# 256 more columns of the first query weights stay in SBUF, and the feed-forward ring is cut into fewer, larger loads

## The chip, the core and the metric

The kernel runs on one core of one Trainium2 chip. The metric is device time in microseconds (us) of one execution, as a median over runs. Beside the times there is one profiled execution, whose trace gives the start and length of each instruction, of each wait and of each load.

## The reference

Two layers with the same weights, for four sequences of one new token each. Each layer is attention over a cache and then a gated feed-forward block:

```python
# B=4, D=640, 32 heads of 128, window of 1024 keys, F=1728, all float32
def _A_ref(x, k_cache, v_cache, wq, wo):
    q = heads_of(x @ wq)
    scores = jnp.einsum("bhqd,bhkd->bhqk", q, k) * (Dh ** -0.5)   # last 1024 keys
    p = _softmax(scores, axis=-1)
    o = jnp.einsum("bhqk,bhkd->bhqd", p, v)
    return merged(o) @ wo

def _B_ref(x, W_gate, W_up, W_down):
    gate = x @ W_gate; up = x @ W_up
    return (gate * (gate > 0) * up) @ W_down

x = x + _A_ref(_layernorm(x), ...);  x = x + _B_ref(_layernorm(x), ...)   # twice
```

Almost all of the work is reading: the last 1024 keys and values of 32 heads and 4 sequences, and the weights, once in each layer.

## The kernel before, in words

All inputs are laid out beforehand as rows of 128 partitions: `heads` (27 of the 32 heads: their columns of W_q, their keys, their values and their rows of W_o, in the order of use), `kept` (the same for the last five heads) and `mlp` (the feed-forward weights in the order of use). A length is counted here in floats per partition; a load of n floats moves 128 rows of n floats.

SBUF holds one large tile, `store` (STORE floats), through which everything streams, and `first_q` (HELD floats), which is loaded once and stays: the first 4608 floats of `heads`, which are the W_q columns of the first group of four heads and four of the five pieces of the second group's. Layer 1 doesn't load them again. The `kept` row stays in `store` as well: layer 0 takes these five heads last and layer 1 takes them first. Layer 0's feed-forward block therefore has little room. It streams its 25920 floats of `mlp` through a ring of seven places, 7040 floats in all: three beyond the kept row (z, f and f+1280 in the code), and four inside it (a = AHEAD, k and k+960 = BACK, q = AWAY). What stood in these four is parked meanwhile: AHEAD in `probs` and the tiles pT, BACK in the PSUM tiles ps, po and y, AWAY in the upper columns of the PSUM tiles pp and m.

A list `plan` has all loads in order. `load()` (L226) issues the next loads on SP's queue as long as the floats they overwrite are no longer marked live; `done()` (L279) unmarks them as TensorE's products have read them. The order of SP's queue is thus fixed by the plan, and each load waits for the product that read its place last. One part of head 17's values comes by small loads of 5, 2 or 1 rows (`limbs`, L238) into the last 2048 floats of `store`.

Groups of heads follow one another: `query`, `query_out` and `query_turned` make the query (TensorE, VectorE, TensorE), `scores` and `softmax` the weights, `values` and `project` the output. `normalized` and `deviation` (L378, L391) are the layer norm: the first gives the centered x in xT, the second the factor rstd, with a product over the partitions (`mean`) ahead of a square root.

The feed-forward block is `forward` (L585). `gate(j)` multiplies one of four pieces of W_gate and W_up (j = 3 first, with 128 columns to a product, then 0, 1, 2 with 256) into `gus[j]`, two halves of the tile pp in turn. `gated(j)` takes the rectified gate by ScalarE and the product with up by VectorE out of it, `hidden(j)` turns that, and `down(j)` multiplies by W_down into y. `fill` and `busy` (L361, L354) are products of the identity with itself into po that nobody reads; in layer 0's feed-forward block they stand at fixed places of TensorE's order.

Of the kernel before, what the change touches and what calls it, by code (L numbers as in the profile page):

```python
# [14 lines left out]
P = 128  # L15
# [11 lines left out]
KV = 4096  # L27
# [33 lines left out]
HELD = 4608  # L61
STORE = 50304
# [3 lines left out]
AHEAD = KEPT * D, KEPT * D + 1088  # L66
# [4 lines left out]
FIRST, MOST = 32128, 16064  # L71
LAP = 3 * MOST
SPLIT, PART = 17, 2048
LIMBS = [(half + i, 5, 0, 1536) for i in range(4) for half in (0, 32)] + [(i, 2, 1536, PART) for i in range(3)] + [(3, 1, 1536, PART), (7, 1, 1536, PART)]
# [39 lines left out]
def decode_kernel(ctx: ExitStack, tc: tile.TileContext, x, source, out):  # L114
# [29 lines left out]
    def stretch(layer, lo, end, to):  # L144

        loads = []
        for hi in fewest(lo, end, -(-(end - lo) // MOST))[1]:
            if to + hi - lo > LAP:
                to = 0
            loads.append((lo, hi, to))  # L150
            to, lo = to + hi - lo, hi
        last = next(i for i, (lo, hi, _) in enumerate(loads) if lo < at_part("v", SPLIT) + KV - 512 <= hi)
        for i, (lo, hi, at) in enumerate(loads):
            if last - 3 < i <= last:
                half = (i - last + 1) * 6 + 1
                plan.extend((layer, "limbs", p, p + 1, STORE - PART) for p in range(max(half, 0), half + 6))
            put(layer, "heads", at, lo, hi)
        return to
# [20 lines left out]
    put(0, "kept", k0, k0, k1, v0, v0 + 6656, v1, v1 + KV, v1 + 7168, FRONT)  # L179
    put(0, "kept", 0, 0, len(HEADS[K0]) * D, KEPT * D)  # L180


    f, z, a, q, k = FRONT, STORE - D, AHEAD[0], AWAY[0], BACK[0]
    assert STORE - FRONT == 1280 + 1024 + D
# [4 lines left out]
    for to, n in gu + gu + gu_end + wd:  # L189
        put(0, "mlp", to, lo, lo + n)  # L190
        lo += n
# [8 lines left out]
    for n in 832, 1280, 1024, 2048, 3392:  # L200
        to = put(1, "heads", to, lo, lo + n)
        lo += n
# [14 lines left out]
    cuts = [0, 7040, 12160, GU0 + 3 * GU, WD1 + WD, MLP - 4 * D, MLP - 2 * D, MLP - D, MLP - QUARTER, MLP]  # L217
# [33 lines left out]
    def place(layer, row, lo):  # L251

        if row == "heads" and lo < HELD:
            return first_q, lo, HELD - lo
        most = KV
        if row == "kept" and layer:
            if AHEAD[0] <= lo < AHEAD[1]:
                i = lo - AHEAD[0] - INSIDE
                if i < 0:
                    return probs, 1024 + i, -i  # L260
                return pT[i // P], GAP + i % P, min(P - i % P, AHEAD[1] - lo)
# [146 lines left out]
    def query(layer, g, spread=False):  # L408
# [7 lines left out]
        part_done(layer, "q", g, 0, (KC - 1) * n)  # L416
        c = KC - 1
# [4 lines left out]
        part_done(layer, "q", g, c * n, n)  # L422

# [39 lines left out]
    def values(layer, g, last=False):  # L463
# [30 lines left out]
        if last:  # L494
# [4 lines left out]
            if layer == 0:  # L499
                nc.gpsimd.tensor_copy(pT[0][:, GAP:], store[:, AHEAD[0] + INSIDE:AHEAD[0] + INSIDE + P])  # L500
                rest = AHEAD[1] - AHEAD[0] - INSIDE - P
                nc.vector.tensor_copy(pT[1][:, GAP:GAP + rest], store[:, AHEAD[1] - rest:AHEAD[1]])
# [32 lines left out]
    def attention(layer):  # L535
        gs = order[layer]
        rstd = deviation(normalized())
        table(AF.Exp)
        query(layer, gs[0], True)
        if layer:  # L540
            for t in pT:
                nc.gpsimd.memset(t, 0.0)
# [10 lines left out]
        for before, g, after, then in zip([None] + gs, gs, gs[1:] + [None], gs[2:] + [None] * 2):  # L553
            totals(g)
            turned()
            if layer == 0 and after is None:
                nc.scalar.copy(probs[:, QUARTER:], store[:, AHEAD[0]:AHEAD[0] + INSIDE])
                nc.scalar.copy(ps.rearrange("p j n -> p (j n)"), store[:, BACK[0]:BACK[0] + 1024])
# [26 lines left out]
    def forward(layer):  # L585
# [35 lines left out]
        def down(j, last=False):  # L621
# [4 lines left out]
            for f in range(4 if j < 3 else 1):  # L626
# [108 lines left out]
```

## Time and profile before

| | |
|---|---|
| median of 3 runs | 729.53 us (729.47 to 729.63) |
| the profiled execution's own time | 729.74 us |
| its span in the trace | 727.9 us |
| TensorE (PE) busy | 450.0 us (62%) |
| VectorE (DVE), ScalarE (ACT) busy | 70.5 us, 54.5 us |
| DMA: SP's queue | 13392 packets, 310.37 MB |

The profiled execution's time is 1.8 us more than its span, and 0.2 us more than the median. PE is TensorE's matmuls, PEld its weight loads; SPq is the instruction that issues a load on SP. A view of windows cuts the span into stretches and gives for each the busy time of the engines, the clock that was granted to TensorE (1.00 is full), the mean busy share of the 16 DMA engines, and what they moved in GB/s. Records of successive packets overlap by a few ns, so that a full share reads 1.00 to 1.05. The chain of waits goes back from the last instruction to what released each step. A line such as L276 is a helper's (`product`): its tiles tell which product it is.

### The profile page before, as it was taken

To read this page: it belongs to the slowest core of one execution; us is meant where nothing else is said; L and a number is where in the kernel's file an instruction comes from. 1 tells how busy PE (TensorE), PEld (TensorE's weight loads), DVE (VectorE), ACT (ScalarE), POOL (GpSimd) and SP (SyncE) were. 2 spreads that over 40 slices of the span, in tenths; PEclk is the share of its full clock that TensorE was granted. 3 is DMA by queue.
4 is the path that set the end of the run, shared out by engine and by line. 5 is a ranking of instruction groups with operands and counts; after the bars stand their busy time and mean duration, and the time that the engine had idled before them with its cause. 6 is when DMAs were issued, how large, how long until landed. Compare 5 with 4: busy or idle time off the path is not lost.

```text
span 727.9 us, 8368 instructions
## 1 busy us (share of the span) xinstructions
PE 450.0 (62%) x3824; PEld 146.9 (20%) x3824; DVE 70.5 (10%) x217; ACT 54.5 (7%) x102; POOL 2.4 (0%) x14
## 2 busy tenths in 40 slices
PE   3546565654645574619868896475756556558576
PEld 1111111111111121103334241021211012102123
DVE  2010001000010000001111211000000010001011
ACT  2000000000000000000412210000000000000100
POOL 0000000000000000000000000000000000000000
PEclk9567888887777787759999999677777878769989
DMA  9999999999999999999999999999999999999997
GB/s 409 444 394 447 440 444 434 412 435 444 443 428 416 421 457 418 444 422 426 418 414 412 426 431 452 429 441 433 434 423 440 438 436 417 441 444 423 425 420 312
DMA packets 13442, 310.91 MB, mean 427 GB/s; under 512 B 1576, under 2 KB 1916, under 8 KB 7136
## 3 DMA queue, kind: packets, MB, share of 16 engines
q1 hardware_dynamic: 13392, 310.37, 99.2%
q8 instruction: 30, 0.49, 0.2%
q14 instruction: 4, 0.03, 0.0%
q10 hardware_dynamic: 16, 0.01, 0.0%
HBM read 310.32 MB, written 0.05 MB: 426 GB/s over the span
## 4 chain that ended last, share of the span: by engine, by line
DMA 77%; PE 20%; DVE 1%; issue 1%; SPq 1%; ACT 0%; DVEq 0%; ACTq 0%
DMA store<-in_heads 62%; DMA store<-in_kept 9%; PE ps L276 8%; DMA store<-in_mlp 6%; PE po L276 6%; PE m L276 2%; PE y L276 1%; PE pp L276 1%; PE pp L461 1%; PE po L490 0%; PE m L432 0%; SPq L238 0%; PE po L358 0%; PE m L521 0%; PE m L512 0%
## 5 line engine op out<-in xcount | busy, mean ns | idle before, releaser
L276 PE MATMUL po<-store,pT 128*16 128x512 f32 x1026 | 157.9, 711 | 120.9 <-DMA store<-in_heads 115.2
L276 PE MATMUL ps<-store,qT 128*4 128x512 f32 (+2 forms) x998 | 152.7, 698 | 101.0 <-DMA store<-in_heads 80.7
L276 PEld LDWEIGHTS po<-store,pT 128*16 128x16 f32 x1026 | 33.4, 109 | 229.5 <-DMA store<-in_heads 126.7
L276 PEld LDWEIGHTS ps<-store,qT 128*4 128x4 f32 x998 | 30.8, 94 | 204.3 <-DMA store<-in_heads 91.8
L457 ACT ACTIVATE probs<-ps,nm 128x1024 f32<-128x1024 f32 x17 | 18.9, 1113 | 334.6 <-DVE nm L453 334.6
L453 DVE TENSOR_REDUCE nm<-ps 128x1 f32<-128x1024 f32 x17 | 20.8, 1225 | 233.9 <-PE ps L276 233.9
L276 PE MATMUL m<-store,xT 128*32 128x512 f32 (+3 forms) x146 | 27.9, 580 | 20.8 <-DMA store<-in_heads 20.8
L276 PE MATMUL y<-store,oT 128*4 128x160 f32 x512 | 23.2, 313 | 10.2 <-DMA store<-in_heads 8.9
L508 ACT COPY gates<-po 128x512 f32<-128x512 f32 x16 | 9.4, 586 | 256.5 <-PE po L276 256.5
L276 PE MATMUL pp<-store,xT 128*32 128x256 f32 (+2 forms) x320 | 20.3, 351 | 9.2 <-DMA store<-in_mlp 4.7
L470 DVE COPY pT<-pp 128x32 f32<-128x32 f32 x64 | 10.3, 184 | 143.5 <-PE po L276 126.4
L461 PE MATMUL pp<-sel_sb,probs 128*128 128x128 f32 x144 | 21.3, 297 | 0.0
L461 PEld LDWEIGHTS pp<-sel_sb,probs 128*128 128x128 f32 x144 | 18.7, 156 | 0.0
L514 DVE RECIPROCAL r<-m 128x16 f32<-128x16 f32 x18 | 4.6, 257 | 123.5 <-PE m L512 123.5
L276 PEld LDWEIGHTS y<-store,oT 128*4 128x4 f32 x512 | 12.7, 89 | 18.4 <-DMA store<-in_heads 9.2
L425 DVE TENSOR_SCALAR gates<-m,rstd 128x512 f32<-128x512 f32 (+2 forms) x18 | 12.4, 690 | 27.1 <-PE m L276 27.1
L276 PEld LDWEIGHTS pp<-store,xT 128*32 128x32 f32 x320 | 10.4, 109 | 17.7 <-DMA store<-in_mlp 8.5
L432 PE MATMUL m<-sel_sb,gates 128*128 128x128 f32 x64 | 12.7, 324 | 0.3 <-DVE gates L425 0.3
L276 PEld LDWEIGHTS m<-store,xT 128*32 128x32 f32 x146 | 6.0, 113 | 32.4 <-DMA store<-in_heads 23.3
L521 PE MATMUL m<-sel_sb,gates 128*128 128x128 f32 x72 | 11.9, 288 | 0.8 <-DVE gates L497 0.8
L432 PEld LDWEIGHTS m<-sel_sb,gates 128*128 128x128 f32 x64 | 7.9, 160 | 19.7 <-issue 18.9
L276 PE MATMUL y<-store,gates 128*4 128x160 f32 (+2 forms) x188 | 9.8, 296 | 1.7 <-DMA store<-in_mlp 1.1
(91 smaller groups left out, 135.7 us busy)
## 6 DMA issues: line engine op xcount, KB each, us to landing
store<-in_heads SPq DMA_DIRECT2D x15, 7936.0 KB
store<-in_heads SPq DMA_DIRECT2D x6, 8032.0 KB
store<-in_heads SPq DMA_DIRECT2D x2, 8000.0 KB
store<-in_heads SPq DMA_DIRECT2D x1, 7872.0 KB
store<-in_heads SPq DMA_DIRECT2D x1, 7424.0 KB
store<-in_heads SPq DMA_DIRECT2D x1, 7360.0 KB
store<-in_heads SPq DMA_DIRECT2D x1, 7168.0 KB
store<-in_heads SPq DMA_DIRECT2D x1, 6400.0 KB
```

What stands on the lines that cost most here:

```text
L276: nc.tensor.matmul(out[:, a:z], by, t[rows, p:p + z - a], start=start and not a, stop=stop and z == n, **how)
L425: nc.vector.tensor_scalar(gates[:, :len(HEADS[g]) * P], qp.pop(g), rstd, SCALE, op0=ALU.mult, op1=ALU.mult)
L432: nc.tensor.transpose(qt[:, i], gates[:, i * P:(i + 1) * P], ident)
L453: nc.vector.tensor_reduce(nm[g], to.rearrange("p j n -> p (j n)"), axis=AX.X, op=ALU.max, negate=True)
L457: nc.scalar.activation(probs, sc.pop(g).rearrange("p j n -> p (j n)"), AF.Exp, bias=nm.pop(g), accum_out=sums[g])
L461: nc.tensor.transpose(pp[:, c // 4, c % 4 * P:c % 4 * P + P], probs[:, c * P:(c + 1) * P], ident)
L470: nc.vector.tensor_copy(to, pp.rearrange("p j (c x) -> p (j c) x", c=4)[:, :, i:P:32])
L508: nc.scalar.copy(gates, po)
L514: nc.vector.reciprocal(r[g], so.rearrange("p (b i) -> p i b", b=B)[:, :SIDE])
L521: nc.tensor.transpose(ot[:, 127 * b:127 * b + P], gates[:, b * P:(b + 1) * P], ident)
```

## The change

- `first_q` holds 4864 floats in place of 4608, and `store` is 256 floats shorter. Layer 1's stream of `heads` begins 256 floats later, so 131072 bytes are read once less.
- Layer 0's feed-forward ring has six places (1280, 1408, 1152, 960, 768, 1280 floats: 6848) in place of seven (7040). AHEAD is 64 floats longer; 32 floats of it are parked in qT.
- The loads of `heads`, `kept` and `mlp` are 85 in place of 91, with `first_q`'s own; the small loads of `limbs` are 24 in place of 26, and stand six and six ahead of two large loads in each layer.
- The gates of j = 0 and 2 are summed in po (columns 256 to 511), those of j = 3 and 1 in pp. Layer 0 parks 384 floats of BACK in columns 128 to 511 of po, by lines that are not changed, so that 256 of them (of head 29's values) come back to layer 1 as gate sums.
- In layer 0's feed-forward block the products nobody reads go away between the gates and in W_down's first two pieces (`down(3)`, `down(0)`). In their place one stands ahead of each product of a gate with which a load begins; it goes to the PSUM tile m that isn't in use.
- The first query of a layer has its last piece behind the product over the partitions of `deviation`, no longer all of it.

```diff
-HELD = 4608
-STORE = 50304
+HELD = 4864
+STORE = 50048
-AHEAD = KEPT * D, KEPT * D + 1088
+AHEAD = KEPT * D, KEPT * D + 1152
-FIRST, MOST = 32128, 16064
+FIRST, MOST = 32000, 16000
...
-    gu = [(z, D), (f, 1280), (f + 1280, 1024), (a, 1088), (k, 960), (k + 960, 768), (q, 1280)]
-    gu_end = [(f, 1280), (f + 1280, 1024), (z, D), (a, D + 256)]
-    wd = [(k, 960), (k + 960, D), (q, 1280), *gu_end, (k, D), (k + D, D)]
+    gu = [(f, 1280), (f + 1280, 1408), (a, 1152), (k, 960), (k + 960, 768), (q, 1280)]
+    wd = [*gu[:4], (k + 960, 704), (q, 1280), *gu[:4], (k + 960, D)]
...
-    for to, n in (f, 1280), (f + 1280, 1024), (z, D), (a, 1088), (k, 1728):
+    for to, n in (f, 1280), (f + 1280, 1408), (a, 1152), (k, 1728):
...
         part_done(layer, "q", g, 0, (KC - 1) * n)
+        value = between and between()
+        turn_of[0] ^= value is not None
         c = KC - 1
...
-        rstd = deviation(normalized())
+        ss = normalized()
+        rstd = query(layer, gs[0], True, lambda: deviation(ss))
         table(AF.Exp)
-        query(layer, gs[0], True)
...
-            gus[j] = pp[:, j % 2, :2 * P]
+            gus[j] = pp[:, 0, :2 * P] if j % 2 else po[:, 2 * P:]
             for c in range(KC):
                 for g in range(groups):
                     lo = at + (c * groups + g) * 2 * n
+                    if layer == 0 and j < 3 and any(lo <= a < lo + 2 * n for a, _, _ in held[0, "mlp"]):
+                        fill(1, banks[turn_of[0] ^ 1])
...
-                if j == 3:
-                    fill(1)
-                elif not (last and f > 1):
+                if 0 < j < 3 and not (last and f > 1):
                     busy(1)
-                if j == 0 and f == 1:
-                    fill(2)
...
         go_on()
-        fill(1)
         h = gated(3)
         for j, j1 in (3, 0), (0, 1), (1, 2):
             gate(j1)
             hidden(j, h)
-            fill(1)
             h = gated(j1)
```

The first place is SP's queue, where layer 0's last feed-forward loads give way to layer 1's first loads of `heads`. Before:

```order
L242 DMA store<-in_mlp 128x1280 x2
L242 DMA store<-in_mlp 128x1024
L242 DMA store<-in_mlp 128x640
L242 DMA store<-in_mlp 128x896
L242 DMA store<-in_mlp 128x640 x2
L242 DMA store<-in_heads 128x1280
L242 DMA store<-in_heads 128x1024
L242 DMA store<-in_heads 128x640
L242 DMA store<-in_heads 128x1088
L242 DMA store<-in_heads 128x1728
```

and in the changed kernel:

```order
L241 DMA store<-in_mlp 128x1280 x2
L241 DMA store<-in_mlp 128x1408
L241 DMA store<-in_mlp 128x1152
L241 DMA store<-in_mlp 128x960
L241 DMA store<-in_mlp 128x640
L241 DMA store<-in_heads 128x1280
L241 DMA store<-in_heads 128x1408
L241 DMA store<-in_heads 128x1152
L241 DMA store<-in_heads 128x1728
```

Between the second load of 1280, into f, and the next load into f there were 3840 floats in five loads; now there are 4160 in four.

The second place is TensorE's order at W_down in layer 0 (y<-store is W_down, po<-sel_sb is a product nobody reads). Before, from the end of the gates to the end of `down(0)`:

```order
L365 MATMUL po<-sel_sb 128x128
L276 MATMUL y<-store,probs 4x160 x4
L365 MATMUL po<-sel_sb 128x128
L276 MATMUL y<-store,probs 4x160 x4
L276 MATMUL y<-store,gates 4x160 x4
L358 MATMUL po<-sel_sb 128x128
L276 MATMUL y<-store,gates 4x160 x4
L358 MATMUL po<-sel_sb 128x128
L365 MATMUL po<-sel_sb 128x128 x2
```

and in the changed kernel, for all of `down(3)` and `down(0)` and on into `down(1)`:

```order
L277 MATMUL y<-store,probs 4x160
L277 MATMUL y<-store,probs 4x96
L277 MATMUL y<-store,probs 4x64
L277 MATMUL y<-store,probs 4x160 x6
L277 MATMUL y<-store,gates 4x160
L277 MATMUL y<-store,gates 4x96
L277 MATMUL y<-store,gates 4x64
L277 MATMUL y<-store,gates 4x160 x18
L359 MATMUL po<-sel_sb 128x128
```

The products nobody reads are gone from these two pieces, and stay from `down(1)` on.

More of the change, by code (lines that the diff above doesn't have):

```diff
@@ L70 @@
 HOME = 12864
-FIRST, MOST = 32128, 16064
+FIRST, MOST = 32000, 16000
 LAP = 3 * MOST
 SPLIT, PART = 17, 2048
-LIMBS = [(half + i, 5, 0, 1536) for i in range(4) for half in (0, 32)] + [(i, 2, 1536, PART) for i in range(3)] + [(3, 1, 1536, PART), (7, 1, 1536, PART)]
+LIMBS = [(half + i, 5, 0, 1536) for i in range(4) for half in (0, 32)] + [(i, 2, 1536, PART) for i in range(4)]
 RUNS = [(half, 20, 512 * s, 40 * s + 20 * (half > 0)) for s in range(3) for half in (0, 32)] + [(0, 8, 1536, 120)]
@@ L153, in stretch @@
         for i, (lo, hi, at) in enumerate(loads):
-            if last - 3 < i <= last:
-                half = (i - last + 1) * 6 + 1
-                plan.extend((layer, "limbs", p, p + 1, STORE - PART) for p in range(max(half, 0), half + 6))
+            if last - 2 < i <= last:
+                half = (i - last + 1) * 6
+                plan.extend((layer, "limbs", p, p + 1, STORE - PART) for p in range(half, half + 6))
             put(layer, "heads", at, lo, hi)
@@ L178, in decode_kernel @@
     put(0, "heads", q_end, turn, *mid, heads_end)
-    put(0, "kept", k0, k0, k1, v0, v0 + 6656, v1, v1 + KV, v1 + 7168, FRONT)
+    put(0, "kept", k0, k0, k1, v0, v0 + 6144, v1, v1 + KV, v1 + 7168, FRONT)
     put(0, "kept", 0, 0, len(HEADS[K0]) * D, KEPT * D)
-    f, z, a, q, k = FRONT, STORE - D, AHEAD[0], AWAY[0], BACK[0]
-    assert STORE - FRONT == 1280 + 1024 + D
-    gu = [(z, D), (f, 1280), (f + 1280, 1024), (a, 1088), (k, 960), (k + 960, 768), (q, 1280)]
-    gu_end = [(f, 1280), (f + 1280, 1024), (z, D), (a, D + 256)]
-    wd = [(k, 960), (k + 960, D), (q, 1280), *gu_end, (k, D), (k + D, D)]
+    f, a, q, k = FRONT, AHEAD[0], AWAY[0], BACK[0]
+    assert STORE - FRONT == 1280 + 1408
+    gu = [(f, 1280), (f + 1280, 1408), (a, 1152), (k, 960), (k + 960, 768), (q, 1280)]
+    wd = [*gu[:4], (k + 960, 704), (q, 1280), *gu[:4], (k + 960, D)]
     lo = 0
-    for to, n in gu + gu + gu_end + wd:
+    for to, n in gu + gu + wd:
         put(0, "mlp", to, lo, lo + n)
@@ L199, in decode_kernel @@
     to = AHEAD[1]
-    for n in 832, 1280, 1024, 2048, 3392:
+    for n in 768, 1280, 1024, 2048, 3392:
         to = put(1, "heads", to, lo, lo + n)
@@ L216, in decode_kernel @@
         to = put(1, "heads", to if to + hi - lo <= STORE else 0, lo, hi)
-    cuts = [0, 7040, 12160, GU0 + 3 * GU, WD1 + WD, MLP - 4 * D, MLP - 2 * D, MLP - D, MLP - QUARTER, MLP]
+    cuts = [0, 12160, GU0 + 3 * GU, WD1 + WD, MLP - 4 * D, MLP - 2 * D, MLP - D, MLP - QUARTER, MLP]
     for lo, hi in zip(cuts, cuts[1:]):
@@ L260, in place @@
                     return probs, 1024 + i, -i
-                return pT[i // P], GAP + i % P, min(P - i % P, AHEAD[1] - lo)
+                if i < 2 * P:
+                    return pT[i // P], GAP + i % P, P - i % P
+                return qT, i - 2 * P, AHEAD[1] - lo
             if BACK[0] <= lo < BACK[1]:
@@ L406, in decode_kernel, with query @@
     qp, nm, sums, sc, r, oT = {}, {}, {}, {}, {}, {}
-    def query(layer, g, spread=False):
+    def query(layer, g, spread=False, between=None):
         n = len(HEADS[g]) * P
@@ L422, in query @@
         part_done(layer, "q", g, c * n, n)
+        return value
     def query_out(g, rstd):
@@ L499, in values @@
             if layer == 0:
-                nc.gpsimd.tensor_copy(pT[0][:, GAP:], store[:, AHEAD[0] + INSIDE:AHEAD[0] + INSIDE + P])
-                rest = AHEAD[1] - AHEAD[0] - INSIDE - P
-                nc.vector.tensor_copy(pT[1][:, GAP:GAP + rest], store[:, AHEAD[1] - rest:AHEAD[1]])
+                for i, on in enumerate([nc.gpsimd, nc.vector]):
+                    lo = AHEAD[0] + INSIDE + P * i
+                    on.tensor_copy(pT[i][:, GAP:], store[:, lo:lo + P])
                 free(*AHEAD)
@@ L536, in attention @@
         gs = order[layer]
-        rstd = deviation(normalized())
+        ss = normalized()
+        rstd = query(layer, gs[0], True, lambda: deviation(ss))
         table(AF.Exp)
-        query(layer, gs[0], True)
         if layer:
-            for t in pT:
+            for t in qT, *pT:
                 nc.gpsimd.memset(t, 0.0)
@@ L557, in attention @@
                 nc.scalar.copy(probs[:, QUARTER:], store[:, AHEAD[0]:AHEAD[0] + INSIDE])
+                lo = AHEAD[0] + INSIDE + 2 * P
+                nc.gpsimd.tensor_copy(qT[:, :AHEAD[1] - lo], store[:, lo:AHEAD[1]])
                 nc.scalar.copy(ps.rearrange("p j n -> p (j n)"), store[:, BACK[0]:BACK[0] + 1024])
```

## The prediction

> **What bounds the kernel now.** I read the page first: the span, the DMA slices, the queue and the chain.
>
> ```profile
> span 727.9 us, 8368 instructions
> DMA  9999999999999999999999999999999999999997
> q1 hardware_dynamic: 13392, 310.37, 99.2%
> DMA 77%; PE 20%; DVE 1%; issue 1%; SPq 1%; ACT 0%; DVEq 0%; ACTq 0%
> ```
>
> The packets of SP's queue fill 99.2% of 16 DMA engines' span, and no slice but the last falls under 9. So a gain must come from fewer bytes, fewer packets, or the little time in which an engine had none. Where that may be is read by stage, from the view of windows (the last two columns are DMA share and GB/s):
>
> ```profile
> 0.00:340.00 340.00, 185.63 (x1380) 54.66 (x1381) 28.41 (x84) 18.34 (x31) 1.77 (x11) 0.77 1.00 431
> 340.00:365.00 25.00, 21.28 (x220) 8.77 (x219) 4.38 (x17) 8.39 (x15) 0.29 (x1) 1.00 0.99 418
> 365.00:386.00 21.00, 14.54 (x202) 7.91 (x206) 2.51 (x9) 2.07 (x7) 0.00 (x0) 1.00 1.02 413
> 386.00:396.00 10.00, 9.83 (x143) 4.22 (x142) 0.99 (x3) 1.74 (x5) 0.00 (x0) 1.00 1.02 410
> 396.00:413.00 17.00, 15.12 (x156) 5.76 (x149) 4.38 (x10) 5.13 (x11) 0.36 (x2) 1.00 1.03 420
> 413.00:620.00 207.00, 133.83 (x1016) 41.02 (x1012) 19.33 (x57) 10.74 (x18) 0.00 (x0) 0.81 1.01 435
> ```
>
> With large loads the engines move 435 GB/s (413 to 620 us). From 340 to 413, where layer 0's ring and layer 1's first small loads run, it is 410 to 420 at the same full share: smaller packets, not empty queues, are most of the difference. The view of DMA, over 339 to 413 and then over 413 to 620, gives the numbers (packets, MB, share):
>
> ```profile
> DMA packets 6283, 30.80 MB, mean 416 GB/s; under 512 B 704, under 2 KB 704, under 8 KB 5568
> q1 hardware_dynamic: 6275, 30.68, 100.7%
> q8 instruction: 6, 0.10, 0.5%
> ...
> q1 hardware_dynamic: 2010, 89.89, 100.4%
> ```
>
> Outside the ring the queue is deep. The chain in order of time has these loads from issue to landing (start, us, what), the first three of heads or kept loads and the last the end of the program:
>
> ```profile
> 199.04 36.92 DMA store<-in_heads
> 283.36 41.80 DMA store<-in_kept
> 461.89 49.62 DMA store<-in_heads
> 693.76 30.76 DMA store<-in_mlp
> ```
>
> A load of 16000 floats is 8.2 MB and takes 18.8 us at 435 GB/s, so each of these stood behind one or two others. In these stages a load can be issued 10 us later and nothing is lost.
>
> **The end.** The windows of the last microseconds:
>
> ```profile
> 720.00:721.00 1.00, 0.61 (x20) 0.21 (x8) 0.00 (x0) 0.00 (x0) 0.00 (x0) 1.00 0.96 398
> 721.00:722.00 1.00, 0.29 (x11) 0.26 (x14) 0.00 (x0) 0.00 (x0) 0.00 (x0) 1.00 0.95 383
> 722.00:723.00 1.00, 0.98 (x32) 0.53 (x20) 0.00 (x0) 0.00 (x0) 0.00 (x0) 1.00 0.78 302
> 723.00:724.00 1.00, 0.57 (x20) 0.41 (x24) 0.33 (x1) 0.00 (x0) 0.00 (x0) 1.00 0.45 168
> 724.00:725.00 1.00, 0.86 (x24) 0.28 (x14) 0.00 (x0) 0.00 (x0) 0.00 (x0) 1.00 0.13 33
> ```
>
> The engines don't finish together: the shares missing from 720 to 724 are 0.04 + 0.05 + 0.22 + 0.55 = 0.86 us, and about 0.4 of the half microsecond after, so the mean engine ends some 1.2 us before the last. The last one sets the end; after its landing at 724.5 come 3.4 us (to 727.9) of products, copies and the store of the result, which the change leaves alone. An engine that is ahead may run dry for a while and cost nothing.
>
> **The change part by part.**
>
> *Bytes.* 256 floats on 128 partitions are 131072 bytes, read once less: at 435 GB/s 0.30 us, shared by all 16 engines alike, the last one too.
>
> *Loads.* 91 large loads become 85. The price of one besides its bytes: the 30.80 MB of 339 to 413 us would take 70.8 us at 435 GB/s and took 74, so 3.2 us more. The instruction fetches (q8) have 0.5% of it, 0.4 us. The other 2.8 us are shared by 6275 / 144 = 43.6 loads (128 packets of data and 16 that signal), 0.064 us each if no engine ever ran dry, and less by what dry engines took. That is seen directly in two windows of 2 us in that stage:
>
> ```profile
> 392.00:394.00 2.00, 1.00 1.00 376
> 400.00:402.00 2.00, 1.00 0.98 386
> ```
>
> Against the stage's 416 GB/s they lack 0.19 and 0.14 us. With some more in the windows beside them I put 0.6 us on dry engines and 0.05 us on a load; the bounds are 0 and 0.064. Six loads: 0.30 us (0 to 0.38). The two small loads of `limbs` that go, and the other split of the rest over two layers, are 2 or 1 rows of 512 floats; I cost them at nothing (at most 0.1 us on one engine).
>
> *The ring.* Six places of 6848 floats for seven of 7040: 192 floats are 0.23 us at 416 GB/s less lead, and a place can only be loaded when all of it has been read, 1408 floats at most now, 1280 before: 0.16 us. Lead there is. The chain in order of time has two loads of the ring, and steps of TensorE beside them; the line below it is the issue of the result's store:
>
> ```profile
> 368.46 1.19 PE pp L276 x19
> 369.66 6.99 DMA store<-in_mlp
> ...
> 377.38 7.58 DMA store<-in_mlp
> ...
> 386.43 0.42 PE po L365 x2
> ...
> 388.96 0.39 PE y L276 x8
> 389.35 0.26 PE po L358
> ```
>
> ```profile
> 725.39 0.35 SPq L632 DMA_DIRECT2D out_x<-probs  x1
> ```
>
> The two loads are of 1088 and 896 floats, 1.3 and 1.1 us of transfer. A lone store of the result, issued at 725.39 with the program's end at 727.9, bounds issue and completion by 2.5 us. So 3.2 and 4.0 us of the 7 were a queue of earlier loads: the engines had work for that long. Losing 0.4 us of it starves no engine that sets the end. The tightest place is the load of `heads` into f: before, five loads of 3840 floats lie between it and the one it overwrites, and once that one has landed two steps of W_down with their unread products follow (0.39 + 0.26 us each by the chain's two last rows). Now f's last reader also needs the first floats of the 1408 behind it, so 2752 floats, 3.4 us, remain in the queue while one step of 0.65 us and an issue of 0.33 us are due: some 2.4 us of lead. I take no change; the bounds are the 0.6 us of dry engines gone, and as much again added.
>
> *Products.* In layer 0's feed-forward block (lines of 360 to 396 us; x counts passes, two to an unread product):
>
> ```profile
> L276 PE MATMUL pp<-store,xT 128*32 128x256 f32 x100 | 10.1, 388 | 2.9 <-DMA store<-in_mlp 1.7 <-DVE gates L606 0.7 <-DVE probs L606 0.4
> L358 PE MATMUL po<-sel_sb 128*128 128x128 f32 x14 | 4.2, 320 | 0.0
> L365 PE MATMUL po<-sel_sb 128*128 128x128 f32 x18 | 3.9, 309 | 0.0
> ```
>
> Gates in two tiles take away the waits for `gated` (0.7 + 0.4 us of TensorE). Four unread products of L358 and three of L365 leave `down(3)` and `down(0)`: by 0.26 us and the chain's 0.42 us about 2.3 us of TensorE's order. Thirteen are added before gates, ahead of a product that waits for its load: 13 x 0.42 = 5.5 us if nothing hid them. It does: a load of 1280 floats takes 1.6 us, its five gate products about 0.65 us (the chain has 19 passes in 1.19 us), with the unread one 1.05. All this moves TensorE, which has lead, so I cost it at nothing on the path. The query's last piece behind `mean` frees AHEAD's neighbours some tenths sooner, at nothing too.
>
> *Sum.* 0.30 + 0.30 = 0.60 us off the profiled execution's 729.74 gives 729.1. That execution is 0.2 above the median, so the median becomes 729.53 - 0.60 = 728.93, say **728.9 us**. Its own range runs from 0.30 (loads free) to 0.30 + 0.38 + 0.6 = 1.28 us off, and to 0.6 less gain: 728.25 to 729.5.
>
> *The skill.* The Trainium skill, "DMA: Bandwidth & Descriptors", section "Anatomy of one DMA", fits a fixed 2.0 us per DMA beside its bytes (for another issuing path), most of it the wait for the write's receipt. Were that paid on the path, eight loads fewer would give an estimated 16 us. The rows above give 0.064 us at most, because the next load's packets run meanwhile; the rule holds for a lone load.
>
> **The rivals.**
>
> *A. TensorE's chain through the ring sets the end.* The page's chain runs through TensorE, VectorE and ScalarE for most of 385 to 435 us. If that were the path, the waits for `gated` (1.1 us) and the unread products (2.3 us) would come off too: 728.9 - 3.4 = 725.5. Against it: DMA shares of 1.02 and 1.03 there, and only 0.3 us that can be pointed at. 8%.
>
> *B. Loads priced like lone ones.* 8 loads x 2 us (a lone one has 2.5 by the store above): 713. No row bears it out; 1%.
>
> *C. TensorE's clock falls in the ring.* It was 1.00 from 340 to 413 us, and 0.81 on average behind it. With the unread products gone, TensorE idles longer for loads. At half clock a step of W_down with its unread product is 1.30 us against 0.80 us of load (640 floats at 410 GB/s): 8 steps late by 0.5 each, and gates of 2.1 us against 1.6, 13 times, late by 0.5 as well: 10.5 us, less the 5.6 us of lead in the two places (3.2 and 2.4): 4.9 us onto the forecast, 733.8. It decides from a step longer than 0.8 us. Against it: a load lands every 1.6 us or so, so no long idle stretch arises, and before, an idle stretch of nearly that length left the clock full (the bracket is TensorE's idle time ahead). 6%.
>
> ```profile
> 371.85 0.16 PEld L276 LDWEIGHTS pp<-store,xT 128*32 128x32 f32 x8 [1.55 <-DMA store<-in_mlp]
> ```
>
> The Trainium skill, "TensorE: Matmul & The Clock Gate", Part 1, has the clock halved after an idle window of about 3.4 us; the trace of before shows full clock with this wait of 1.55 us in this stage, which agrees.
>
> *D. Another engine ends last.* The 30 instruction fetches of 16 KB take their time on single engines: 0.2% of 16 spans is 23 us, 0.8 us for each. One more on the last engine takes the gain back:
>
> ```profile
> q8 instruction: 30, 0.49, 0.2%
> ```
>
> 728.9 + 0.8 = 729.7. The program has nearly the same number of instructions, so their places should hold; 10%.
>
> **How the numbers follow.** Forecast 75%, A 8%, B 1%, C 6%, D 10%. About 0.2%, 1.5 us, is what a measurement of this kernel can tell from no change. The forecast and D lie inside it but for a tail of the forecast of 2% below and 1% above. Faster: 8 + 1 + 2 = 11%. Slower: 6 + 1 = 7%. Same: 82%. The range 728.2 to 729.9 holds the forecast's own and D.
>
> **What would show it.** The queue's MB falls by 0.13 and its packets by about 860; the share of 16 engines stays at 99%; the windows of the ring keep a share near 1.00 and clock 1.00; the last load of `mlp` lands near 723.9 instead of 724.5, and 3.4 us follow. The idle time of the 256-column gate products for `gated` goes. The prediction is wrong if a window between 340 and 413 us falls well under 400 GB/s, or if the gain is some microseconds, which would make TensorE's chain the path.

## The result, and the profile after

The changed kernel takes 730.97 us (median of 21 runs, 729.96 to 732.42), the kernel before 729.59 in the same comparison (729.36 to 730.87): the ratio is 1.0018, interval 1.0011 to 1.0025. It is slower by 1.4 us, just inside the 0.2% of the prediction, which had it 0.6 us faster with a range up to 729.9. The profiled execution after took 730.47 us, that of before 729.74.

The page of the changed kernel, in the lines that the prediction showed of before (span, DMA share by slice, SP's queue with packets, MB and share, the chain):

```profile
span 728.7 us, 8380 instructions
DMA  9999999999999999999999999999999999999997
q1 hardware_dynamic: 12528, 310.24, 99.1%
DMA 76%; PE 22%; DVE 1%; issue 1%; SPq 0%; ACT 0%; DVEq 0%; ACTq 0%
```

Bytes and packets came as forecast, 0.13 MB and 864 packets fewer at a share of 99%. Yet the last load of `mlp` landed later. The chain has, right behind that landing, before and then after (start, us, what):

```profile
724.52 0.04 issue
```

```profile
725.34 0.04 issue
```

These 0.8 us of the two profiled executions are lost at one place. The windows of the changed kernel (busy time of PE, PEld, DVE, ACT and POOL, then clock, DMA share, GB/s):

```profile
340.00:365.00 25.00, 21.58 (x230) 8.93 (x222) 4.53 (x18) 8.54 (x15) 0.51 (x2) 1.00 0.99 420
365.00:386.00 21.00, 19.86 (x226) 10.82 (x228) 2.88 (x11) 2.10 (x7) 0.00 (x0) 1.00 1.02 417
386.00:396.00 10.00, 7.71 (x125) 3.45 (x124) 0.49 (x2) 1.64 (x4) 0.00 (x0) 1.00 1.02 410
396.00:413.00 17.00, 15.06 (x146) 5.84 (x148) 4.38 (x10) 5.11 (x10) 0.46 (x3) 1.00 1.00 394
413.00:620.00 207.00, 129.98 (x1022) 39.82 (x1014) 19.33 (x57) 10.75 (x18) 0.00 (x0) 0.83 1.01 435
```

The ring is as fast as before or faster (418, 413, 410 GB/s became 420, 417, 410). From 396 to 413, the start of layer 1, 420 became 394: 26 GB/s over 17 us are 0.44 MB, 1.0 us at 435 GB/s. The share hardly shows it: 1.03 became 1.00. In windows of 4 us (clock, share, GB/s), first before, then after:

```profile
400.00:404.00 4.00, 1.00 1.00 397
404.00:408.00 4.00, 1.00 1.04 425
```

```profile
400.00:404.00 4.00, 1.00 0.96 365
404.00:408.00 4.00, 1.00 1.04 378
```

With the same share of 1.04 the engines moved 425 GB/s and 378. The sizes of the packets aren't the reason: if each packet took the median time of its size between 340 and 420 us, the bytes of after would flow at 419 GB/s from 404 to 408. Some packets are recorded as far longer than that (last section), so a full share isn't a fed engine.

What is late there is seen in the chain in order of time. Before:

```profile
397.06 0.24 PE m L374 x8
397.30 1.26 PE m L276 x19
398.58 0.63 DVE gates L425
...
400.11 3.17 PE pp L276 x25
```

After:

```profile
396.98 0.84 PE m L277 x8
...
398.40 0.27 ACT rstd L395
398.72 1.05 PE m L277 x10
...
400.62 5.33 PE pp L277 x48
```

In these rows `mean` is the product of L374 before and of L375 after, and the queries are those of L276 and L277 into m. Before, `mean` comes first and the queries of layer 1's first two groups follow on TensorE without a gap. After, `mean` stands behind four query pieces; the square root starts at 398.40 (397.43 before), and the second group's query, which sums into the PSUM bank that the root reads, waits for it until 398.72. The scores (pp) begin 0.5 us later. SP's issues follow these products. Two successive loads of `heads` on SP's queue (start, us from the first issue to the end of the second), before and after:

```profile
398.57 0.80 SPq L242 DMA_DIRECT2D store<-in_heads  x2
```

```profile
398.50 1.63 SPq L241 DMA_DIRECT2D store<-in_heads  x2
```

The second, 1280 floats, is issued at 399.80 in place of 399.02, and the two loads behind it (1024 and 2048) start at 401.69 in place of 401.18:

```profile
401.18 1.19 SPq L242 DMA_DIRECT2D store<-in_heads  x2
```

```profile
401.69 1.19 SPq L241 DMA_DIRECT2D store<-in_heads  x2
```

### The profile page after: what moved, and what is told of

The parts are those of the page before. It is cut to its first block, busy times and chain, and to the rows that moved or that the text cites. A ratio compares the mean times of both kernels' runs of the same rounds, so it can differ in the third digit from the quotient of the medians.

```text
span 728.7 us, 8380 instructions
## 1 busy us (share of the span) xinstructions
PE 452.5 (62%) x3836; PEld 147.8 (20%) x3836; DVE 70.5 (10%) x217; ACT 54.5 (7%) x102; POOL 2.7 (0%) x16
## 4 chain that ended last, share of the span: by engine, by line
DMA 76%; PE 22%; DVE 1%; issue 1%; SPq 0%; ACT 0%; DVEq 0%; ACTq 0%
DMA store<-in_heads 61%; PE ps L277 10%; DMA store<-in_kept 8%; DMA store<-in_mlp 7%; PE po L277 5%; PE y L277 2%; PE m L277 1%; PE pp L277 1%; PE m L436 1%; PE pp L465 0%; PE m L366 0%; PE m L525 0%; PE po L359 0%; PE m L516 0%; PE y L405 0%
## 5 line engine op out<-in xcount | busy, mean ns | idle before, releaser
L277 PE MATMUL po<-store,pT 128*16 128x512 f32 (+2 forms) x1028 | 155.1, 706 | 128.0 <-DMA store<-in_heads 122.8
L277 PE MATMUL ps<-store,qT 128*4 128x512 f32 (+5 forms) x996 | 155.8, 695 | 104.6 <-DMA store<-in_heads 82.3
L277 PEld LDWEIGHTS po<-store,pT 128*16 128x16 f32 x1028 | 33.5, 108 | 233.1 <-issue 112.2
L277 PEld LDWEIGHTS ps<-store,qT 128*4 128x4 f32 x996 | 30.2, 94 | 210.7 <-DMA store<-in_heads 93.5
L277 PE MATMUL m<-store,xT 128*32 128x512 f32 (+3 forms) x146 | 27.5, 576 | 20.5 <-DMA store<-in_heads 20.3
L277 PE MATMUL y<-store,oT 128*4 128x160 f32 x512 | 22.2, 302 | 1.1 <-DVE oT L529 1.1
L465 PE MATMUL pp<-sel_sb,probs 128*128 128x128 f32 x144 | 19.5, 281 | 0.0
L465 PEld LDWEIGHTS pp<-sel_sb,probs 128*128 128x128 f32 x144 | 17.1, 146 | 0.0
L277 PE MATMUL po<-store,xT 128*32 128x256 f32 (+2 forms) x170 | 14.5, 399 | 0.4 <-DMA store<-in_mlp 0.2
L277 PEld LDWEIGHTS y<-store,oT 128*4 128x4 f32 x512 | 12.7, 87 | 8.7 <-issue 3.8
L277 PEld LDWEIGHTS m<-store,xT 128*32 128x32 f32 x146 | 6.4, 116 | 31.2 <-DMA store<-in_heads 22.0
L277 PE MATMUL y<-store,gates 128*4 128x160 f32 (+3 forms) x188 | 9.6, 296 | 3.7 <-DMA store<-in_mlp 3.1
L277 PE MATMUL m<-first_q,xT 128*32 128x512 f32 (+2 forms) x46 | 8.6, 718 | 4.7 <-DMA first_q<-in_heads 3.5
```

Of the source, the lines that this page charges most:

```text
L277: nc.tensor.matmul(out[:, a:z], by, t[rows, p:p + z - a], start=start and not a, stop=stop and z == n, **how)
L465: nc.tensor.transpose(pp[:, c // 4, c % 4 * P:c % 4 * P + P], probs[:, c * P:(c + 1) * P], ident)
```

## The experiments

Theory L (lateness): the new query order makes the factor rstd and the loads behind it late, and this late feeding is the loss. Rivals: R (ring), the new ring's geometry loses it (the place of 1408 floats above all, which comes free late); P (products), the new products cost it, that is the gates in two tiles and the other places of the products that nobody reads ("unread products" below). Each time is a median, with its difference from the kernel before in the same comparison.

| kernel | us | against before |
|---|---|---|
| changed kernel | 730.97 | +1.4 |
| changed, old query | 729.87 | +0.4 |
| before, new query | 730.90 | +1.4 |
| new ring alone | 731.86 | +2.3 |
| changed, place of 1408 cut in two | 730.91 | +1.4 |
| the same, old query | 730.19 | +0.6 |
| new ring alone, place cut in two | 732.13 | +2.5 |
| before, 2 products ahead of the query | 730.74 | +1.2 |
| before, 4 products ahead of the query | 731.96 | +2.4 |
| changed, `mean` into y | 730.67 | +1.1 |
| before, new products alone | 730.52 | +1.0 |
| the same, down(0)'s unread ones kept | 729.53 | -0.1 |
| changed, down(0)'s unread ones kept | 730.90 | +1.3 |
| changed, old query, gates in one tile | 735.52 | +6.0 |
| new ring, without unread products in down(3), down(0) | 731.41 | +1.9 |
| new ring, gates in two tiles | 730.41 | +0.9 |
| changed, old query, no products ahead of gates | 729.67 | +0.1 |
| before, gates in two tiles | 729.91 | +0.4 |

In each kernel with gates in po the parked floats of those columns are lost, as in the changed kernel. An interval is about 0.7 us to either side (1.0 for the ring alone), so that differences under a microsecond between two rows are only suggestive.

### One edit back, one edit alone

The changed kernel with the old query order:

```diff
-        ss = normalized()
-        rstd = query(layer, gs[0], True, lambda: deviation(ss))
+        rstd = deviation(normalized())
         table(AF.Exp)
+        query(layer, gs[0], True)
```

> The changed kernel with one part undone: the first query stands behind the whole of deviation again, as before. Theory L (late factor): in the changed kernel the product over the partitions stands behind four query pieces on TensorE, so the square root for rstd starts at 398.40 us instead of 397.43, the second group's query waits for it (398.72, because it sums into the PSUM tile that the square root reads), and SP's loads behind it are issued 0.5 to 0.8 us later, in a stage where the queue is only some 2.4 us deep. Undoing it gives the forecast back: 729.0 (728.7 to 729.4). Theory R (ring): the six larger places starve the engines by themselves, the query is beside the point: 730.3 to 731. Theory P (products): the unread products' places do it: 730.3 to 731.

The kernel before with the new order (the reverse diff):

> The kernel before with one part added: the last piece of the first query behind the product over the partitions. Theory L: rstd comes 0.9 us later here too, and the loads behind it 0.5 to 0.8 us; before's lead there is 2.6 to 4.2 us instead of 2.4, so part of it is absorbed: 729.9 to 730.9. Theories R and P: no change, 729.4 to 729.7.

Measured: 729.87 (ratio 1.0009, 1.0000 to 1.0018) and 730.90 (1.0018, 1.0009 to 1.0027). The second is where theory L had it, and R and P had no change. The first lies between the ranges of L and of its rivals: the order is most of the loss, but without it the forecast doesn't come back. The order costs 1.0 us on the new ring (1.4 less 0.4) and 1.4 on the old, so it is the larger part of the result. With the old order on the new ring the dip is another one, earlier:

```profile
396.00:400.00 4.00, 1.00 0.95 356
400.00:404.00 4.00, 1.00 1.00 400
404.00:408.00 4.00, 1.00 1.05 428
```

The new ring and bytes with the old query and the old products:

```diff
-            gus[j] = pp[:, 0, :2 * P] if j % 2 else po[:, 2 * P:]
+            gus[j] = pp[:, j % 2, :2 * P]
...
-                if 0 < j < 3 and not (last and f > 1):
+                if j == 3:
+                    fill(1)
+                elif not (last and f > 1):
                     busy(1)
...
```

> The changed kernel with old query order, old gate tiles (both in pp) and old unread products: what is left is the 256 floats that stay, the six places, the large and small loads' cut. Theory L: 729.0 (728.7 to 729.5), the saved bytes and loads. Theory R: as the changed kernel or worse, 730.5 to 731.5. Theory P: 729.0.

Measured: 731.86 (1.0032, 1.0019 to 1.0045). The ring, forecast at nothing, loses 2.3 us when nothing else is changed, more than any of the theories had for it, and the new products give most of that back (729.87 with them). In W_down its TensorE waits for no load, and nor did the kernel before. The groups of 384 to 396 us, before and then with the ring alone (busy, mean ns, idle ahead):

```profile
L276 PE MATMUL y<-store,gates 128*4 128x160 f32 (+2 forms) x100 | 5.8, 294 | 0.0
```

```profile
L277 PE MATMUL y<-store,gates 128*4 128x160 f32 (+4 forms) x100 | 6.0, 294 | 0.1
```

So TensorE had no lead there on either ring. The shorter one has less in the queue behind that chain, and from 392 to 400 us the engines move 372 and 334 GB/s, where before they moved 397 and 412.

The place of 1408 floats as two, for the ring's loads of `mlp` and for those of `heads` behind them (the diff shows the latter), in the changed kernel, with the new query, with the old, and on the ring alone:

```diff
-    for to, n in (f, 1280), (f + 1280, 1408), (a, 1152), (k, 1728):
+    for to, n in (f, 1280), (f + 1280, 768), (f + 2048, 640), (a, 1152), (k, 1728):
```

> The changed kernel with the place of 1408 floats cut in two, 768 and 640, and its loads with it: four loads more in layer 0 and one more in layer 1, no other difference. Theory R: smaller places are freed sooner, the loads of 392 to 400 us come up to 1 us earlier: 729.4 to 730.2. Theories L and P: five loads at 0.05 us more, 0.2 to 0.3 us slower than the changed kernel: 731.0 to 731.4.

> The changed kernel with two of its edits put back: the place of 1408 floats is cut into 768 and 640, and the query goes behind mean again. Theories L and R together (late query, and a place of 1408 that comes free late): both dips, at 394 to 398 and at 402 to 406 us, are gone, 400 GB/s or more in each window, and the time is 728.9 to 729.3, under the kernel before. If the cut of the place only moves the dip on, as it did under the late query: 729.7 to 730.1, the time with the old query alone.

> The kernel before with only the bytes and the ring changed, as in the run of the ring alone, but the place of 1408 floats cut into 768 and 640: 7 places, 6848 floats, old query, old products. Theory R (the ring alone lost 2.3 us by the place of 1408, which comes free late): 729.3 to 730.2 us, with 400 GB/s or more in the windows from 394 to 400. If it lost them by the 192 floats that the ring is shorter, or by the waits for gates in one tile: 731.3 to 731.9, and the windows stay near 370 and 300.

Measured: 730.91, 730.19 and 732.13: no gain in any of the three. The dip from 394 to 400 us goes (410 and 429 GB/s in the windows from 392 with the old query), but then 400 to 404 has 377 and 404 to 408 has 390. What the queue gets sooner it lacks later. So the size of the place isn't the cause with the new products. On the ring alone it is less sure: in that profiled execution the clock also fell, to 0.73 from 372 to 376 us, which may hide a gain.

### How much lateness costs

The kernel before, with two unread products ahead of the second group's query in layer 1, and then with `fill(4)`; all else is untouched:

```diff
         query_out(gs[0], rstd)
+        waits[0] = layer == 1
+        fill(2)
         query(layer, gs[1])
```

> The kernel before with two unread products (0.44 us each on TensorE) ahead of the second group's query in layer 1; query order, ring and gates are the old ones. Theory L (what costs is that the loads behind this query are issued later, whatever makes it late): the load of 1280 floats is issued at 399.6 to 399.9 us in place of 399.02, the windows from 402 to 406 us fall to 320 to 370 GB/s, and the time is 730.4 to 730.9 us. Rival Q (the loss came from something else in the new query order: its bank, ScalarE, the order on TensorE): loads later, time 729.4 to 729.8.

> The same with four unread products, 1.76 us. Theory L: the load of 1280 is issued at about 400.5 to 400.8 us, each further microsecond of lateness is a microsecond of dry engines, and the time is 731.3 to 731.9 us. If the loss were a single fixed price of a late first packet, the time would be that of two products, 730.4 to 730.9. Rival Q: 729.4 to 729.8.

Measured: 730.74 (1.0014, 1.0005 to 1.0023) and 731.96 (1.0028, 1.0017 to 1.0039): 0.88 us of TensorE cost 1.2 us, 1.76 cost 2.4, so no slack is seen. With four products, SP's two issues and the windows:

```profile
398.63 2.40 SPq L242 DMA_DIRECT2D store<-in_heads  x2
```

```profile
400.00:404.00 4.00, 1.00 0.99 343
404.00:408.00 4.00, 1.00 0.90 289
```

This shows the price without the new order: lateness of these loads is paid about in full. Whether more than in full isn't told, since the intervals are 0.4 to 1.7 us and 1.2 to 2.8. Two products make the loads somewhat later than the new order does (the 1280 floats are issued at 400.08, in the changed kernel at 399.80) and cost about as much.

Which part of the lateness counts was tried by taking the wait at the bank away. `mean` for rstd goes into an unused column of y:

```diff
-        rstd = query(layer, gs[0], True, lambda: deviation(ss))
+        rstd = query(layer, gs[0], True, lambda: deviation(ss, yy[:, 480:481]))
```

> The changed kernel with mean's product for the factor in an unused column of the tile y, so that the second group's query needn't wait until the square root has read the bank that it sums into. Theory L, with this wait as half of the lateness: the second group's products begin 0.4 us sooner, the load of 1280 is issued at 399.3 to 399.5 us in place of 399.80, the windows from 402 to 406 rise to 380 or more, and the time is 730.1 to 730.6 us. If the wait is not what makes it late: issued at 399.7 to 399.9, and 730.8 to 731.2.

Measured: 730.67 (1.0014, 1.0006 to 1.0023). SP's two issues take 0.99 us, near the 0.80 before, but the two loads behind them start at 401.56, against 401.69 after and 401.18 before. The windows of this run:

```profile
398.42 0.99 SPq L241 DMA_DIRECT2D store<-in_heads  x2
...
401.56 1.19 SPq L241 DMA_DIRECT2D store<-in_heads  x2
```

```profile
400.00:404.00 4.00, 1.00 1.02 394
404.00:408.00 4.00, 1.00 0.97 303
```

The wait went, and the load of 1280 floats was issued at 399.09, sooner than the 399.3 to 399.5 expected. But the dip didn't go, as it should have (380 GB/s or more from 402 to 406, where 353 were measured): it moved on, and from 404 to 408 it is deeper, 303 GB/s against 378. The time missed the 730.1 to 730.6 expected by a hair, and 0.3 us can't be told from nothing. So the wait at the bank isn't most of what costs. What stays late is the factor itself, and with it the scores, whose products free the places of the following loads; that this is the part that counts is argued and not shown.

### The products

The kernel before with the new products alone, and the same with the unread products of down(0) kept:

```diff
-                if 0 < j < 3 and not (last and f > 1):
+                if j < 3 and not (last and f > 1):
                     busy(1)
```

> The kernel before with only the new products: gates in two PSUM tiles and the other places of the unread products; old ring, old query, old loads. If these are worth something by themselves (they took 2.0 us off the new ring): the window of 392 to 394 us rises from 376 to 400 GB/s or more, and the time is 728.8 to 729.2. If they only repair what the new ring had lost, or if TensorE had lead there: 729.4 to 729.7. If the unread products ahead of the gates' loads delay something: 730.0 or more.

> The kernel before with the new products, but the four unread products of down(0) kept. With all of the new products alone, the granted clock fell to 0.50 from 392 to 394 us, after 387 to 391 us in which TensorE was busy 2.0 of 4 us. Theory C (that loss is the clock, and the clock falls for want of these four): the clock stays 1.00, the load of 1024 into f is issued near 392.6 us in place of 393.45, and the time is 729.4 to 729.8 us, that of the kernel before. Rival (gates in two tiles, or the products ahead of their loads, cost it themselves): 730.2 to 730.8.

Measured: 730.52 (1.0014, 1.0002 to 1.0026) and 729.53 (0.9999, 0.9990 to 1.0008). The first shows rival C in its trace (PE busy, clock, share, GB/s):

```profile
388.00:390.00 2.00, 0.73 (x16) 1.00 1.00 412
390.00:392.00 2.00, 1.73 (x26) 0.85 1.04 418
392.00:394.00 2.00, 2.00 (x28) 0.50 1.04 409
```

TensorE waits for loads in W_down, its granted clock falls to 0.50, its steps take longer and the loads that depend on them are issued later (1024 floats into f at 393.45 in place of 392.62). With the four products kept the clock stays at 1.00 and the loss is gone. The eleven runs without them lie in two groups, 4 from 729.5 to 729.7 and 7 from 730.5 to 734.0, as if the clock fell in some executions only; one of them is profiled, so that this is argued and not shown.

In the changed kernel, where the profile has the full clock from 340 to 413 us, the same edit was tried:

> The changed kernel with the four unread products of down(0) kept. Its profiled execution had the full clock, with TensorE busy 2.1 of 4 us from 387 to 391. If its clock falls in executions that no profile shows, they are some of its loss: 729.9 to 730.5 us, with a smaller spread. If not: 730.7 to 731.2. If the four hold W_down up instead: 731.3 or more.

Measured: 730.90. The clock is not its loss.

On the new ring the new products take 2.0 us off. They were taken apart in four ways: gates in one tile again; the unread products of down(3) and down(0) left out and none put ahead of the gates; gates in two tiles with the old unread products; two tiles and none ahead of the gates.

```diff
-            gus[j] = pp[:, 0, :2 * P] if j % 2 else po[:, 2 * P:]
+            gus[j] = pp[:, j % 2, :2 * P]
```

> The changed kernel with the old query and with the gates in the two halves of one tile again; the unread products stay at their new places. On the new ring the new products took 731.86 down to 729.87 us. Theory T (it is the unread products that left W_down, which TensorE ran back to back there from 385 to 395 us): 729.6 to 730.2 us. Rival G (it is the waits for gates in one tile): 731.3 to 731.9.

> The run of the ring alone (731.86 us), with the seven unread products of down(3) and down(0) left out, and nothing put in ahead of the gates; gates in one tile. Theory T: TensorE waits for loads again in W_down, the first load of heads into f is issued near 391.3 us in place of 392.00, the windows from 392 to 400 rise to 380 or more, and the time is 729.7 to 730.3 us; if the clock falls there, as it did with the new products alone on the old ring, 730.5 to 731.2. Rival G: 731.3 to 731.9 and the windows stay.

> The run of the ring alone (731.86 us) with the gates in two PSUM tiles; unread products at their old places, old query. Theory G (the new ring loses by the waits of the next gate's products for the gate before, in one tile): 729.6 to 730.2 us, and the first load of heads into f is issued near 391.3 us in place of 392.00. If the unread products in W_down lose it too, so that only both edits together help: 730.8 to 731.9.

```diff
-                    if layer == 0 and j < 3 and any(lo <= a < lo + 2 * n for a, _, _ in held[0, "mlp"]):
-                        fill(1, banks[turn_of[0] ^ 1])
```

> The changed kernel with the old query and without the thirteen unread products ahead of the gates' loads; none in down(3) and down(0) either; gates in two tiles. If the thirteen are hidden behind loads, as the prediction had it, and the clock holds: 729.5 to 730.0 us, as with them (729.87). If they hold the clock up: it falls to 0.5 in some stretch between 368 and 396 us, and the time is 731 or more.

> The kernel before with the gates in two PSUM tiles and nothing else. By what the prediction said of TensorE's lead on the old ring, and by the run with all new products and the clock held (729.53): 729.4 to 729.7 us. If the waits for gates in one tile cost on the old ring too: 728.9 to 729.3.

Measured: 735.52 (1.0078, 1.0066 to 1.0089), 731.41 (1.0030, 1.0021 to 1.0040), 730.41 (1.0014, 1.0004 to 1.0024), 729.67 (1.0000, 0.9991 to 1.0009), and on the old ring 729.91 (1.0006, 0.9997 to 1.0015). Theory T, that the unread products in W_down alone were the ring's loss, fell: without them it is 731.41. Two tiles alone bring 731.86 to 730.41, about three quarters of the way to the 729.6 to 730.2 expected; with the unread products of W_down and those between the gates gone too it is 729.67. The groups of 360 to 396 us with one tile and the moved products show the worst case:

```profile
L277 PE MATMUL pp<-store,xT 128*32 128x256 f32 (+3 forms) x166 | 14.1, 348 | 2.7 <-DVE probs L614 1.4 <-DVE gates L614 0.9 <-DVE xT L389 0.5
L366 PE MATMUL m<-sel_sb 128*128 128x128 f32 x26 | 6.3, 326 | 0.0
```

With two tiles and without the thirteen:

```profile
L277 PE MATMUL po<-store,xT 128*32 128x256 f32 (+3 forms) x90 | 8.3, 364 | 4.7 <-DMA store<-in_mlp 4.7
L277 PE MATMUL pp<-store,xT 128*32 128x128 f32 (+3 forms) x76 | 5.0, 327 | 1.8 <-DMA store<-in_mlp 1.2 <-DVE xT L389 0.5
```

In the first the gates' products wait 2.3 us for the gate before (1.4 + 0.9) and never for a load: TensorE is the later one. The thirteen products are paid there, 4.1 us between 731.41 and 735.52 in the same comparison, and that is net of four unread products between the gates that only the run of 731.41 still has. That run, with one tile and without the thirteen:

```profile
L277 PE MATMUL pp<-store,xT 128*32 128x256 f32 (+2 forms) x166 | 12.2, 347 | 6.2 <-DMA store<-in_mlp 4.6 <-DVE gates L612 0.6 <-DVE xT L389 0.5
```

Its gates wait 4.6 us for loads, and still little of the thirteen was hidden in that; why isn't shown. In the run with two tiles the gates wait 5.9 us for loads (4.7 + 1.2), and thirteen products of 0.42 us, 5.5 us, fit into that: with them 729.87, without 729.67.

No kernel beat the one before by what can be measured.

## Why the prediction was wrong

**The step that failed** is "The query's last piece behind `mean` frees AHEAD's neighbours some tenths sooner, at nothing too". What it counted on is small (the pieces begin at 396.98 in place of 397.14, and SP's next load at 398.50 in place of 398.57), but `mean` itself went behind four pieces, the square root started 1.0 us later, a bank made the second query wait for it, and the scores came 0.5 us later. I followed what the piece frees, and not what the delayed `mean` holds up. Price: 1.0 us on the new ring, 1.4 on the old. That the sum came out only 1.4 us above the kernel before is luck, since three errors stand against one another: +1.0 us for the order, +2.9 for the ring with its bytes and loads (0.6 less forecast, 2.3 more measured), and -2.0 for the products.

**Why lateness was dear** is an older error. The part on the bound, "smaller packets, not empty queues, are most of the difference", holds as an average: with the median time of each packet size (159 ns at 4096 bytes, 196 at 5120, 309 at 8192) the bytes of the kernel before from 340 to 413 us would flow at 416 GB/s, and SP's queue moved 414. But an average doesn't say that every place has lead. The two delays show no slack at the start of layer 1 for the loads behind the query; there the 397 GB/s from 400 to 404, where the median times give 413, were already a sign. The clause "the engines had work for that long", worked out from two loads at 369 and 377 us, was carried over to a place where it isn't true.

**The ring at nothing** failed as a step by itself: 2.3 us (1.4 to 3.3 by the interval of its ratio), outside the bounds of 0.6, and more still if the bytes and loads in this run saved anything. The 2.4 us of lead there were worked out from bytes in the queue, one of TensorE's steps and an issue. But it is TensorE's chain that the loads wait for, and in W_down this chain had no lead even before (0.0 us of waits for loads): on the shorter ring it still runs without a gap, with 0.23 us less of bytes in the queue to cover it. Why 0.23 us become 2.3 us of time the runs don't say.

**Products at nothing** failed on the new ring with the other sign: 2.0 us off, so that ring, products, bytes and loads together come to 0.4 us more, not 0.6 less. "All this moves TensorE, which has lead" was the wrong half, by the row of 0.0. The covering load was the condition of the other, as the step said; it holds with two tiles (5.9 us of waits for 5.5 us of products) and not with one, where at least 4.1 us of the forecast "5.5 us if nothing hid them" were paid. That the waits for `gated` are off the path was right on the old ring (all new products with the clock held 729.53; two tiles alone 729.91, with a fall of the clock in its profile, see the last section) and wrong on the new one.

**Bytes and loads**, 0.60 us, came into the counters but not into the time. The best of the new ring, 729.67, is 0.1 above the kernel before where the forecast had 728.9. Why is open. One reading would be the queue: the 256 floats that stay are taken from `store`, and the loads that can be issued between the ring and the scores hold 6336 floats in place of 6592, 0.30 us less just where lateness is paid. The profiled execution of that best kernel (two tiles, none ahead of the gates) doesn't bear it out, since nothing is lost from 400 to 408 (the first two rows, 397 and 425 GB/s before). What it shows is the end:

```profile
400.00:404.00 4.00, 1.00 1.01 400
404.00:408.00 4.00, 1.00 1.06 431
720.00:721.00 1.00, 1.00 0.92 367
721.00:722.00 1.00, 1.00 0.86 341
722.00:723.00 1.00, 1.00 0.65 250
723.00:724.00 1.00, 1.00 0.30 106
```

The shares missing from 720 to 724 are 1.27 us, before 0.86, while the last load lands at 724.38 in place of 724.52. So in this one execution the mean engine is done some 0.4 us sooner against the last one, and most of the saving lies on engines that weren't last. The prediction had it shared by all 16, "the last one too". One execution of each kernel doesn't show whether that is the rule.

**The rivals.** A, TensorE's chain on the path, was dismissed for the kernel before. Its gain didn't come on the old ring (729.91 without the waits for `gated`), but the two delays show that at the start of layer 1 this chain had no slack even there. On the new ring it holds, through the gates' one tile. B was rightly dismissed. C, the clock, did not happen in the changed kernel (1.00 from 340 to 413, and 730.90 with more unread products), but did with the new products on the old ring, at 1.0 us and not 4.9. The argument against it, "no long idle stretch arises", isn't enough: the clock fell though no stretch there was longer than 1.1 us. The row of 1.55 us beside it is the idle time of a weight load; TensorE's own products waited 1.07 us there. D, another engine ending last, isn't needed for the changed kernel, whose loss is seen from 396 to 413.

**What would show it** served: the list said that the prediction is wrong if a window between 340 and 413 falls well under 400 GB/s, and that is where it broke, at 365 and 378.

## What to carry to other kernels

When a product is moved behind others, follow what it holds up, through banks and engines to the next load issued, and not only what the move sets free. In a stage of small loads read GB/s against the best of its neighbours, since the busy share stays at 1.00 while engines starve, and price lateness by putting two and then four unread products there: the pair of runs told it to about 0.7 us. Edits to a ring and to the engine that empties it belong together: the ring alone lost 2.3 us here, the products alone 1.0 on the old ring, both together 0.4.

## What the runs showed of the hardware

A starved DMA engine shows as long packets. Matching packets to engines by size and by the end they follow (some few per cent can't be matched), 29 of the 40 packets from 390 to 412 us that took over 100 ns more than the usual one of their size, in the kernel before with the new query, were the first of a load on their engine, and they had 14.7 of 17.7 us of the excess. A second way of matching gives 27 and 14.1 us. In the kernel before the excess is 7 us, and 4.0 to 4.4 of it lie on first packets. In the changed kernel it is 17 us, where the two ways differ (10.9 and 5.8 us on first packets), so that there it is open how much lies on them. Single packets took 1.5 us and more, where the usual ones take 0.16 us (4096 bytes) to 0.31 (8192). The recorded share hides this: in the changed kernel from 404 to 408 us the packets of SP's queue would fill 0.89 of the engines by their median times, and by the records they fill 1.02.

The granted clock fell without a long idle stretch. With the new products alone on the old ring TensorE was busy 2.0 of the 4 us from 387 to 391, its longest wait 1.09 us, and the clock went to 0.50 near 391.4 us for some 3 us; with two tiles alone on the old ring, 2.3 of 4 us from 368 to 372 were followed by 0.54:

```profile
368.00:372.00 4.00, 2.27 (x36) 1.00 1.02 411
372.00:376.00 4.00, 4.00 (x39) 0.54 1.02 421
```

The changed kernel was busy 2.1 of 4 us from 387 to 391 and kept the full clock. The traces tell more of this edge. In each of the 19 traces the changes of the clock lie on a grid of 3.41 us, whose place differs from execution to execution. In the window of the grid just ahead of each of the 583 falls TensorE was busy at most 0.55 of the time; in the 1889 windows at full clock with no fall behind them, at least 0.41. The two falls above had 0.55 and 0.50 in that window, the changed kernel 0.55 in its window up to 389.3 us. So here a window about half idle was enough for a fall. As the grid's place differs, the same waits may make such a window in one execution and not in the next, which fits the two groups of times above. The Trainium skill, "TensorE: Matmul & The Clock Gate", Part 1, halves the clock after an idle window of about 3.4 us; the prediction found the trace in agreement with it. The 3.4 us agree with the grid of 3.41, but these two rows don't agree with it as a rule on single idle stretches.
